# Two transformer-mixer layers on one core: VectorE's steps dealt by rank, its value products placed when ready, partial sums fetched at once

## The chip, the core and the metric

The kernel runs on one core of a Trainium2 chip. The metric is the device time of one execution in microseconds (us); lower is better. The core's engines each work through their own instructions in order and wait for one another by semaphores: TensorE (PE in the profile) multiplies matrices, ScalarE (ACT) computes activation functions, VectorE (DVE) does elementwise work and statistics, GpSimd (POOL) here computes one small power, and SyncE (SP) issues the data transfers (DMAs). Matmul results land in PSUM, all else is kept in SBUF.

## The reference

Two layers, each an attention block and a token-mixing MLP with residuals, on a sequence of 2048 tokens with 640 features:

```
def _A_ref(x, wqkv, wo):                      # H = 32 heads of Dh = 20
    q, k, v = split(x @ wqkv)                 # each (B, H, S, Dh)
    p = softmax(einsum("bhqd,bhkd->bhqk", q, k) * Dh ** -0.5)
    o = einsum("bhqk,bhkd->bhqd", p, v)
    return merge_heads(o) @ wo

def _B_ref(x, w1, b1, w2, b2):                # mixes over the 2048 tokens
    h = layernorm(x)
    u = gelu(einsum("bsd,sf->bdf", h, w1) + b1)     # F = 1536
    return transpose(einsum("bdf,fs->bds", u, w2) + b2)

x = A_x
x = x + _A_ref(layernorm(x), A_wqkv, A_wo)
x = x + _B_ref(layernorm(x), B_w1, B_b1, B_w2, B_b2)
x = x + _A_ref(layernorm(x), A_wqkv, A_wo)
x = x + _B_ref(layernorm(x), B_w1, B_b1, B_w2, B_b2)
```

(B is 1; `split`, `merge_heads` and `transpose` stand for the reshapes.) Inputs are bfloat16.

## The kernel before

**Attention (`attention`, L274).** The work of a layer is cut into 32 blocks: four query blocks of 512 queries (`qb`) by eight groups of four heads (`g`). A block has 16 units, one for each tile of 128 keys (`kt`). A unit is four chunks, one per head, each 128 keys by 512 queries. The keys 5 and 11 of every block (`D_KTS`) are VectorE's; the chunks of the other 14 units are laid end to end into tiles of three and two chunks alternately (`TW`), 717 tiles a layer.

The loop at L741 goes over these tiles and writes down the order of the instructions; nothing is reordered on TensorE or VectorE after that (`pe`, `dv` chain them). For tile `t` it emits: the scores of tile `t+1` (`emit_S`; two-chunk tiles are repeated twice, to keep TensorE busy, unless fill work is planned); ScalarE's exponential of tile `t` (`emit_exp`, L405); value products (`emit_PV`, L678) of the units whose exponentials are done; what `d_at` lists for VectorE's units; VectorE's waiting steps (`run_threads`); and matmuls of other work, the fills (`emit_fills`). Scores have two PSUM buffers, one for the three-chunk and one for the two-chunk tiles, so the scores of tile `t+2` wait for the exponential of tile `t`. The accumulator of the value products, the buffer of VectorE's scores and that of the fills (`misc`) exist once each.

**VectorE's units.** `emit_D` multiplies one chunk of scores into `Sd` and evicts it as an integer (`du<-Sd`, L416). After two chunks a thread (`d_steps`) makes the exponential of both by bit operations in three steps (`dm`, L426; `de`, L429; the product `du<-dm,du`, L433). The product of the unit with the values takes two operands, `du` and `de`. The chunks of a block's two units are emitted every second tile (`D_STEP`), and the value product six tiles after the last chunk of its unit (`D_PV_LAG`).

**Threads.** Threads are generators: each step names a cost and a delay, and `run_threads` lets them run in the order in which they were started as long as the cost fits what is left of 0.75 (`DVE_ROOM`) in the tile. `finish_thread` emits all that is left of one at once. Three kinds exist: the exponentials; the normalization of a finished block (`normalize`, L435: a transpose T out of the accumulator at once, then reciprocal, product and transpose into `attnT`; the next block's normalization finishes the thread before it emits its own T); and the layernorms of the mixer (`do_ln2`, L472: twice two statistics, mean and epsilon, a power on GpSimd, and the apply; the next token tile finishes the thread of the one before).

**Fills** are taken from a queue: key and query projections of later blocks (L254), the output projection of a finished query block (L577; that of the last query block in batches over heads 0-3, 4-6 and 7, L608), and the first mixer matmul over the tokens that are done (L552), whose partial sums go to memory (`upar`, then `uacc`). What is left of them after the last tile runs in the tail, followed by the layernorms of the last four token tiles (`emit_ln2_staged`, L503).

**Mixer (`mixer_mm1`, L782).** It multiplies the last four token tiles by their part of w1 in four passes of three 128-row groups, adds the partial sums (`ua`, fetched from `uacc` per pass into four buffers, L806; added at L833 into one of two buffers) and applies Gelu (L837). The w2 loads (L845) and the second matmul (L894) follow, in layer 0 together with the projections of the next layer.

## Time and profile before

| | us |
|---|---|
| median of 3 runs (2023.59 to 2029.77) | 2025.27 |
| profiled execution | 2016.61 |
| its span, first to last instruction | 2014.8 |

| stretch of the span (us) | length | TensorE busy | VectorE busy | ScalarE busy |
|---|---|---|---|---|
| start, projections: 0 to 47.7 | 47.7 | 34.9 | 36.6 | 25.5 |
| attention, layer 0: 47.7 to 913.9 | 866.2 | 752.8 | 601.1 | 821.4 |
| tail: 913.9 to 938.3 | 24.4 | 9.7 | 19.0 | 1.7 |
| first mixer matmul: 938.3 to 962.8 | 24.5 | 18.9 | 10.6 | 12.7 |
| second, with projections: 962.8 to 1049.5 | 86.7 | 83.7 | 49.3 | 27.8 |
| attention, layer 1: 1049.5 to 1916.3 | 866.8 | 757.5 | 601.0 | 820.5 |
| tail: 1916.3 to 1940.7 | 24.4 | 9.3 | 19.1 | 2.0 |
| first mixer matmul: 1940.7 to 1960.2 | 19.5 | 17.7 | 10.7 | 12.8 |
| second: 1960.2 to 2014.8 | 54.6 | 49.6 | 16.2 | 11.6 |

A row of a group in the profile has the line, engine and operation, what it writes and reads, shapes and count; then the busy time, the mean duration in ns, and the idle time of the engine just ahead of these instructions with what ended it. A row of the waits names the engine and line that waited, the one waited for, the total, the number of waits and the longest. A row of the timeline has the start, the duration, the instruction, and in brackets the idle time before it and its releaser. TensorE's matmuls overlap, so that rows follow each other faster than their durations.

### The profile page before, as it was taken

How to read it: one execution, taken by the hardware profiler on the slowest of the kernel's cores; microseconds unless marked ns; L12 is line 12 of the kernel's file. 1: busy time of each engine (PE TensorE's matmuls, PEld its weight loads, DVE VectorE, ACT ScalarE, POOL GpSimd, SP SyncE). 2: the span in 40 equal slices, each digit the busy share in tenths (PEclk: the TensorE clock that was granted, in tenths of full speed). 3: DMA queues.
4: the chain of work that ended last, by engine and by line, in shares of the span. 5: the costliest groups of instructions: out<-in, count | busy, mean ns of one | idle time of the engine just before them, and what ended most of it. 6: DMA issues, size and time to landing. Idle time of an engine off the chain costs nothing.

```text
span 2014.8 us, 33568 instructions
## 1 busy us (share of the span) xinstructions
PE 1734.0 (86%) x12988; PEld 624.4 (31%) x13128; DVE 1363.7 (68%) x2544; ACT 1736.2 (86%) x1575; POOL 63.2 (3%) x106
## 2 busy tenths in 40 slices
PE   7989888888898998885999898888888989888869
PEld 4222222222232322322542222222222332223235
DVE  7676668665876677766556676685668766777662
ACT  5999998999899998993339999989999999889932
POOL 2000001000000000000000000000000000000000
PEclk9999999999999999997999999999999998989979
DMA  6000000000111111234620000010001111122355
GB/s 135 1 1 1 1 11 30 1 1 1 36 47 47 47 36 57 65 93 148 208 86 1 1 1 1 17 38 1 1 1 53 54 48 42 36 74 61 104 157 180
DMA packets 113599, 96.98 MB, mean 48 GB/s; under 512 B 46752, under 2 KB 99104, under 8 KB 113440
## 3 DMA queue, kind: packets, MB, share of 16 engines
q1 hardware_dynamic: 109824, 94.82, 15.4%
q8 instruction: 102, 1.67, 0.4%
q0 software_dynamic: 3616, 0.01, 0.3%
q14 instruction: 57, 0.47, 0.1%
HBM read 63.35 MB, written 31.46 MB: 47 GB/s over the span
## 4 chain that ended last, share of the span: by engine, by line
ACT 35%; PE 30%; DVE 20%; issue 13%; DMA 1%; POOL 0%; DVEq 0%; ACTq 0%; SPq 0%; POOLq 0%
ACT P L405 35%; PE S L384 9%; PE acc L678 6%; PE y L894 5%; DVE du L416 4%; PE Sd L384 2%; PE misc L552 2%; PE misc L254 2%; PE pp L245 2%; DVE du L433 1%; DVE T L444 1%; DVE attnT L452 1%; DVE qod L223 1%; DVE qev L223 1%; DVE T L449 1%
## 5 line engine op out<-in xcount | busy, mean ns | idle before, releaser
L405 ACT ACTIVATE P<-S 128x1024 bf16<-128x1024 f32 (+1 forms) x1434 | 1642.5, 1270 | 93.0 <-PE S L384 87.3
L384 PE MATMUL S<-qev,KT 64*128 64x512 bf16 (+1 forms) x2464 | 597.7, 387 | 67.1 <-ACT P L405 53.4
L384 PE MATMUL S<-qod,KT 64*128 64x512 bf16 (+1 forms) x2376 | 586.5, 387 | 61.0 <-ACT P L405 51.3
L416 DVE TENSOR_SCALAR du<-Sd 128x512 int16<-128x512 f32 x512 | 354.2, 692 | 277.6 <-PE Sd L384 247.7
L384 PEld LDWEIGHTS <-KT 64*128 64x128 bf16 (+1 forms) x5352 | 262.5, 93 | 649.1 <-issue 573.4
L678 PE MATMUL acc<-P,Vaug 128*32 128x512 bf16 x3584 | 364.0, 395 | 23.1 <-DVE T L444 22.0
L678 PEld LDWEIGHTS <-Vaug 128*32 128x32 bf16 x4608 | 111.8, 93 | 310.0 <-issue 302.8
L433 DVE TENSOR_TENSOR du<-dm,du 128x1024 bf16<-128x1024 bf16 x256 | 177.3, 693 | 8.8
L552 PE MATMUL misc<-h2st,w1st 128*128 128x320 bf16 x576 | 127.2, 314 | 11.6 <-DVE qod L223 6.2
L192 POOL TENSOR_TENSOR rstd<-veps,mhalf 128x1 f32<-128x1 f32 x96 | 59.6, 621 | 1877.6 <-DVE veps L190 1835.0
L429 DVE TENSOR_SCALAR de<-du 128x1024 int16<-128x1024 int16 x256 | 109.3, 427 | 8.8
L426 DVE TENSOR_SCALAR dm<-du 128x1024 int16<-128x1024 int16 x256 | 109.3, 427 | 8.7
L444 DVE STREAM_TRANSPOSE T<-acc 128x512 f32<-128x512 f32 x64 | 45.9, 717 | 100.2 <-PE acc L678 97.0
L384 PE MATMUL Sd<-qod,KT 64*128 64x512 bf16 x256 | 100.5, 392 | 15.0 <-DVE du L416 14.4
L894 PE MATMUL y<-uT,w2s 128*128 128x128 bf16 (+1 forms) x753 | 106.8, 297 | 3.4 <-ACT uT L837 2.6
L384 PE MATMUL Sd<-qev,KT 64*128 64x512 bf16 x256 | 98.8, 386 | 2.6 <-DVE du L416 1.9
L254 PE MATMUL misc<-hh,wq_pad 128*128 128x512 bf16 x262 | 86.2, 396 | 12.5 <-DVE KT L639 7.0
L254 PE MATMUL misc<-hh,wk_pad 128*128 128x512 bf16 x242 | 80.4, 385 | 4.2 <-issue 2.5
L577 PE MATMUL misc<-wo_pad,attnT 128*128 128x128 bf16 (+1 forms) x363 | 74.5, 305 | 10.6 <-DVE qod L223 6.1
L552 PEld LDWEIGHTS <-w1st 128*128 128x128 bf16 x576 | 47.8, 98 | 93.0 <-issue 84.1
L894 PEld LDWEIGHTS <-w2s 128*128 128x128 bf16 x768 | 59.7, 98 | 49.0 <-issue 4.2
L678 PE MATMUL acc<-du,Vaug 128*32 128x512 bf16 x512 | 57.2, 388 | 13.6 <-DVE du L433 13.4
(91 smaller groups left out, 1027.2 us busy)
## 6 DMA issues: line engine op xcount, KB each, us to landing
w2s<-in_B_w_dram SPq DMA_DIRECT2D x16, 768.0 KB
xd<-x1s SPq DMA_DIRECT2D x24, 320.0 KB
upar<-ustg SPq DMA_DIRECT2D x48, 160.0 KB
uai<-upar SPq DMA_DIRECT2D x48, 160.0 KB
uacc<-ustg SPq DMA_DIRECT2D x48, 160.0 KB
x1in<-xd SPq DMA_DIRECT2D x24, 320.0 KB
ua<-uacc SPq DMA_DIRECT2D x24, 320.0 KB
w1st<-in_B_w_dram SPq DMA_DIRECT2D x24, 256.0 KB
```

The lines of the kernel that those rows point to most:

```text
L254: pe(nc.tensor.matmul(t[:, :], lhsT=wpad[:, dt_, g, :], rhs=st.hT[:, dt_, tb * 512:(tb + 1) * 512], start=(dt_ == 0), stop=(dt_ == NDT - 1)))
L384: pe(nc.tensor.matmul(St[:, slot, :], lhsT=KT[r0:r0 + rows, g, kt * 128:(kt + 1) * 128], rhs=q[r0:r0 + rows, :], start=True, stop=True, ti ...
L405: nc.scalar.activation(out=P[:, 0:ncs, :].rearrange("p a b -> p (a b)"), in_=St[:, 0:ncs, :].rearrange("p a b -> p (a b)"), func=ACT.Exp, ...
L416: dv(nc.vector.tensor_scalar(out=u[:, k * 512:(k + 1) * 512], in0=Sd[:, 0, :], scalar1=DBIAS, scalar2=0.0, op0=ALU.add, op1=ALU.max))
L426: dv(nc.vector.tensor_scalar(out=m[:], in0=u[:], scalar1=0x7f, scalar2=0x3f00, op0=ALU.bitwise_and, op1=ALU.bitwise_or))
L429: dv(nc.vector.tensor_scalar(out=e[:], in0=u[:], scalar1=0x7f80, scalar2=0x0001, op0=ALU.bitwise_and, op1=ALU.bitwise_or))
L433: dv(nc.vector.tensor_tensor(out=ub, in0=m[:].bitcast(BF16), in1=ub, op=ALU.mult))
L444: dv(nc.vector.transpose(out=T1[:], in_=acc[:]))
L552: pe(nc.tensor.matmul(t[:, 0:w], lhsT=states[ft]["w"][:, i, :], rhs=hts[i][:, c0:c1], start=(i == 0), stop=(i == ns - 1)))
L577: pe(nc.tensor.matmul(t[:, 0:w], lhsT=attnT[:, ttl * 128:(ttl + 1) * 128], rhs=wo_pad[:, g, c0:c1], start=(g == 0), stop=(g == NG - 1)))
L678: pe(nc.tensor.matmul(acc[32 * j:32 * j + 32, :], lhsT=Vaug[:, o:o + 32], rhs=sl[j], start=first and k3 == 0, stop=done and k3 == len(term ...
L894: pe(nc.tensor.matmul(y[:, 0:w], lhsT=w2s[:, ft, sl * 128:(sl + 1) * 128], rhs=uT[:, ft, c0:c1], start=(ft == 0), stop=(ft == NF - 1)))
```

## The change

It has four parts. Threads get a rank (exponentials 0, normalization 1, layernorm 2), and `run_threads` serves them by rank; the normalization's reciprocal becomes a step of its own, cost 0.25, and its product another, cost 0.7. The value product of VectorE's units has no fixed place: it goes into a tile in which both of the unit's threads had ended by the tile before, if that tile has fewer than three slots taken, and at the latest ahead of the block's last product. In the mixer all twelve partial sums are fetched ahead of the first pass, into twelve buffers, and the sum has three buffers in place of two. Ahead of the staged layernorms one ScalarE instruction with Gelu on one column is added.

```diff
@@ start_thread, step, run_threads
-            def start_thread(gen):
-                th = dict(gen=gen, ready=now[0], cost=0.0, done=False)
+            def start_thread(gen, rank):
+                th = dict(gen=gen, ready=now[0], cost=0.0, done=False, rank=rank, end=0)
...
                 except StopIteration:
                     th["done"] = True
+                    th["end"] = now[0]
                     threads.remove(th)
...
-                for th in list(threads):
+                for th in sorted(threads, key=lambda x: x["rank"]):
@@ normalize
-                    yield 0.9, 0
+                    yield 0.25, 0
                     dv(nc.vector.reciprocal(out=rden[:], in_=T1v[:, :, DH]))
+                    yield 0.7, 0
                     dv(nc.vector.tensor_tensor(out=T2[:], in0=T1v, ...
@@ emit_ln2_staged
+                nc.scalar.activation(out=warm[:, 0:1], in_=items[0][1][:, 0:1], func=Gelu_apprx_tanh, scale=1.0)
@@ the attention loop
-                    at_ += CFG["D_PV_LAG"]
-                    d_at.setdefault(at_, []).append(("PV", b_ * NKT + kt_, 0))
+            d_open = deque()
+            def d_done(n, before):
+                ths = [D_tiles[(n, half)][2] for half in range(2)]
+                return all(th["done"] and th["end"] <= before for th in ths)
...
                 while pv_ready and pv_ready[0][1] <= t - LAGT:
-                    emit_PV(pv_ready.popleft()[0])
+                    n_a = pv_ready.popleft()[0]
+                    if units[n_a][2] == NKT - 1:
+                        while d_open and d_open[0] < n_a:
+                            emit_PV(d_open.popleft())
+                            slots += 2
+                    emit_PV(n_a)
                     slots += 1
+                while d_open and d_done(d_open[0], t - 1) and slots < 3:
+                    emit_PV(d_open.popleft())
+                    slots += 2
                 for (op, n, i_) in d_at.get(t, ()):
-                    if op == "S":
-                        emit_D(n, i_)
-                        slots += 1
-                    else:
-                        emit_PV(n)
-                        slots += 2
+                    emit_D(n, i_)
+                    slots += 1
+                    if i_ == 3:
+                        d_open.append(n)
@@ mixer_mm1
-            uap = m1.enter_context(tc.tile_pool(name=f"uap{layer}", bufs=4))
-            tmpp = m1.enter_context(tc.tile_pool(name=f"utmp{layer}", bufs=2))
+            uap = m1.enter_context(tc.tile_pool(name=f"uap{layer}", bufs=NF))
+            tmpp = m1.enter_context(tc.tile_pool(name=f"utmp{layer}", bufs=3))
+            uas = []
+            for ft in range(NF):
+                ua = uap.tile([128, D], F32, name="ua")
+                nc.sync.dma_start(out=ua[:], in_=uacc_l[ft * 128:(ft + 1) * 128, :])
+                uas.append(ua)
             for fh in range(NPASS):
-                uas = []
-                if MMO > 0:
-                    for ftl in range(FP):
-                        ft = fh * FP + ftl
-                        ua = uap.tile([128, D], F32, name="ua")
-                        nc.sync.dma_start(out=ua[:], in_=uacc_l[ft * 128:(ft + 1) * 128, :])
-                        uas.append(ua)
```

More of the change, by code (lines that the diff above doesn't have):

```diff
@@ L39 @@
     D_STEP=2,
-    D_PV_LAG=6,
     LN_LAG=2,
@@ L420, in emit_D @@
                     D_tiles[(n, half)].append(e)
-                    D_tiles[(n, half)].append(start_thread(d_steps(u, e)))
+                    D_tiles[(n, half)].append(start_thread(d_steps(u, e), 0))
             def d_steps(u, e):
@@ L457, in steps @@
                         enqueue_outproj(qb)
-                last_th["norm"] = start_thread(steps())
+                last_th["norm"] = start_thread(steps(), 1)
             hT_dead = [False]
@@ L500, in steps @@
                         enqueue_mm1_partial(range(8, 12), uacc_l, upar_l)
-                last_th["ln"] = start_thread(steps())
+                last_th["ln"] = start_thread(steps(), 2)
             def emit_ln2_staged(items):
                 assert check_hT_dead()
+                nc.scalar.activation(out=warm[:, 0:1], in_=items[0][1][:, 0:1], func=ACT.Gelu_apprx_tanh, scale=1.0)
                 for i0 in range(0, len(items), 4):
@@ L734, in attention @@
                         d_at.setdefault(at_, []).append(("S", b_ * NKT + kt_, i_))
-                    at_ += CFG["D_PV_LAG"]
-                    assert at_ < t_end, (at_, t_end)
-                    d_at.setdefault(at_, []).append(("PV", b_ * NKT + kt_, 0))
+                assert at_ + 4 < t_end, (at_, t_end)
             LAGT = CFG["PV_LAGT"]
             pv_ready = deque((n, max(chunk_at[(n, j)][0] for j in range(4))) for n in a_units)
+            d_open = deque()
+            def d_done(n, before):
+                ths = [D_tiles[(n, half)][2] for half in range(2)]
+                return all(th["done"] and th["end"] <= before for th in ths)
             emit_S(0, 0)
@@ L762, in attention @@
                 emit_PV(pv_ready.popleft()[0])
+            assert not d_open
             finish_all()
@@ L832, in mixer_mm1 @@
                         tmp = tmpp.tile([128, D], F32, name="utmp")
-                        nc.vector.tensor_tensor(out=tmp[:], in0=big[:, ftl * D:(ftl + 1) * D], in1=uas[ftl][:], op=ALU.add)
+                        nc.vector.tensor_tensor(out=tmp[:], in0=big[:, ftl * D:(ftl + 1) * D], in1=uas[ft][:], op=ALU.add)
                         src = tmp[:]
```

## The prediction

> **What bounds the kernel now.** I read the page first, then the table of waits, then the timeline of one quiet stretch and of the disturbed ones. Both attention stages together hold 1733 of the 2015 us of the span, and in them ScalarE's exponentials are the bound.

> ```profile
> L405 ACT ACTIVATE P<-S 128x1024 bf16<-128x1024 f32 (+1 forms) x1434 | 1642.5, 1270 | 93.0 <-PE S L384 87.3
> L678 PE MATMUL acc<-P,Vaug 128*32 128x512 bf16 x3584 | 364.0, 395 | 23.1 <-DVE T L444 22.0
> ```

> ScalarE is busy for 1642.5 us and idle for 93.0 us ahead of an exponential, nearly all of it because TensorE brought the scores late. So the question of each edit in attention is: does TensorE, which works in the written order, stand still longer or shorter? The table of waits says for whom it stands still:

> ```profile
> PE acc L678 <- DVE T L444: 22.0, 26, 1.9
> PE Sd L384 <- DVE du L416: 16.3, 28, 1.3
> PE acc L678 <- DVE du L433: 13.4, 18, 1.4
> DVE h2st L197 <- POOL rstd L192: 4.4, 6, 0.8
> DVE utmp L833 <- DMA ua<-uacc: 6.6, 4, 4.7
> ```

> The first row is the accumulator that the transpose T has not yet emptied, the third is a value product that waits for VectorE's exponentials (only 18 of 128 such products wait today), the fourth a layernorm emitted in one go, the last the partial sums. Now a quiet stretch with one VectorE score tile, its steps, and the slack there is:

> ```profile
> 386.19 0.39 PE L384 MATMUL Sd<-qod,KT 64*128 64x512 bf16 x1
> 386.62 0.69 DVE L416 TENSOR_SCALAR du<-Sd 128x512 int16<-128x512 f32 x1 [1.14 <-PE Sd L384]
> 387.34 0.43 DVE L426 TENSOR_SCALAR dm<-du 128x1024 int16<-128x1024 int16 x1
> 387.60 0.37 PE L384 MATMUL S<-qev,KT 64*128 64x512 bf16 x1 [0.19 <-ACT P L405]
> 387.81 0.43 DVE L429 TENSOR_SCALAR de<-du 128x1024 int16<-128x1024 int16 x1
> 388.27 0.69 DVE L433 TENSOR_TENSOR du<-dm,du 128x1024 bf16<-128x1024 bf16 x1
> 388.35 0.09 PEld L384 LDWEIGHTS <-KT 32*128 32x128 bf16 x1 [0.42 <-issue]
> 388.94 0.37 PE L384 MATMUL S<-qod,KT 32*128 32x512 bf16 x1 [0.52 <-ACT P L405]
> ```

> ```profile
> 387.44 1.46 ACT L405 ACTIVATE P<-S 128x1536 bf16<-128x1536 f32 x1
> ```

> ```profile
> 389.67 1.48 ACT L405 ACTIVATE P<-S 128x1536 bf16<-128x1536 f32 x1
> ```

> The reader sees that the chain from the score matmul at 386.19 to the finished exponentials takes until 388.96, that TensorE is through its work at 388.35, and that the next three-bank score group runs at 388.94, as soon as its bank is free. It ends near 389.33, and the exponential that needs it starts at 389.67. With 0.10 for the handing over, 0.24 us of slack is left.

> **Part 1, value products "when ready": +115 us.** Before, the product of a VectorE tile stood six tiles behind its last score matmul. In the order of the changed program it stands two tiles behind, at all 128 places (32 blocks, 2 units, 2 layers): the planner calls a tile ready one tile after it has written down the last step. On the chip that step ends 3.6 to 4.0 us after the start of the exponential of its tile (here 388.96, the exponential having started at 385.18), and TensorE gets there earlier: after the group that began at 387.60, at 388.35. So TensorE stops until 389.02. From the first such product to the next score group the timeline has 0.53 us:

> ```profile
> 393.10 0.39 PE L678 MATMUL acc<-du,Vaug 128*32 128x512 bf16 x4
> 393.63 0.38 PE L384 MATMUL S<-qev,KT 32*128 32x512 bf16 x1
> ...
> ```

> That puts the group at 389.55 and the exponential at 390.04 instead of 389.67: 0.37 us, and 0.45 where another product stands ahead of the score matmul. Behind the waiting product there stand on TensorE, in the order listing: nothing at 24 places (0.45 each, 10.8); the next score matmul for VectorE at 24 (+0.33, the step from 385.86 to 386.19: 0.75, 18.0); one to three fill matmuls, often with that score matmul, at 80. Of these, 48 cost about 0.9 (43.2), and at 32 an eviction for a fill (0.49 to 0.75 us) stands on VectorE before the last step, so about 1.35 (43.2). Sum 115 us. Lower bound: the earliest chain (3.57 us) everywhere and the fills half hidden, 70. Upper bound: the 13.4 us of the third row left the exponentials idle for 19 us, 1.43 per us waited; on a mean wait of 0.8 us that is 146. I take 115, since it goes place by place.

> **Part 2, ranks and the split normalization: -31 us.** Before, the three steps rden, T and attnT cost 0.9 in a budget of 0.75, so they never ran by themselves; they were forced out just ahead of the next T (62 of 64 blocks). When VectorE is late, 1.66 us stand in front of T:

> ```profile
> 610.63 0.71 DVE L452 STREAM_TRANSPOSE attnT<-T 128x512 bf16<-128x512 bf16 x1
> 611.45 0.72 DVE L444 STREAM_TRANSPOSE T<-acc 128x512 f32<-128x512 f32 x1
> 612.22 0.40 PE L678 MATMUL acc<-P,Vaug 128*32 128x512 bf16 x4 [1.91 <-DVE T L444]
> ```

> Now they run one or two tiles after their own T, and no T has them in front. The 22.0 us of waits go; exponentials idled some 25 us behind them: -25 (between -29 and -18). The 13.4 us that products waited behind layernorm steps idled the exponentials for 19 us: -19. But with layernorm last, it is unfinished more often when the next token tile arrives, and is then emitted whole: 16 such runs in the listing against 6. Each holds VectorE for two statistics (0.99), mean and epsilon (0.35), the wait for GpSimd (0.73) and the apply (0.61), 2.7 us, often with 0.61 more; queued behind it are the evictions of VectorE's scores, and behind these TensorE. About half stand where a score or step is due within a tile and cost 1 to 2 us: +13 (0 to 26). Sum -31.

> **Part 3, what moves out of the tail: -12 us.** The output projection is enqueued a block earlier, so of its second batch one 128-wide group is left after the last exponential instead of all four tiles, which ran 2.22 us apart at 917.72, 919.94 and 922.16. From attnT's end (916.87) to the last batch at 924.38 that is 7.5 us less 0.5. In their place two partial-sum groups of four matmuls fall into the tail; their two additions (0.49 each) stand in VectorE's layernorm chain: +1.0. Per layer -6, both -12 (-14 to -9). In the loop, 40 fewer repeated score matmuls and 18 more projection matmuls are issued: TensorE has idle time beside them, 0; at most +3.

> **Part 4, partial sums at once, early Gelu table: -7 us.** Before, eight of twelve loads stood on SP behind three w2s loads and the reuse of four buffers; VectorE waited 4.7 us in layer 0. Layer 1, where the table load is early and the waits are 1.4 us, needs 19.4 us from its first matmul (1940.73) to its last Gelu (1960.16); layer 0 needs 24.55. Without waits 18.5 each: -6.0 and -0.9. All twelve now stand ahead of w2s and, for the last eight, behind the two additions in the tail; 3.9 MB at the 204 GB/s of that stage are 19 us, begun some 6 us before the matmuls, and each load is needed over 15 us. Should w2s come late behind them, up to 5 us are lost. The extra ScalarE instruction and table load lie in an 18 us wait: 0.

> **Sum.** +115 - 31 - 12 - 7 = +65 us. The profiled execution took 2016.6 us, so 2082 by it; the median of the runs is 8.7 us above that, so I predict 2089.

> **The clock, a cost outside the sum.** After the 1.91 us stop at 612.22 matmuls took twice as long for 3.4 us (acc at 615.37 took 0.62 us against 0.40), while stops of 0.88 and 0.96 us at 207.8 and 237.0 left them as they were. The 80 places with fills will stop TensorE for 0.8 to 1.5 us; if one in four trips the clock at about 1 us, that is +20. [...]

> **Rivals.** (a) Faster: the steps are in time. If TensorE reached each product 0.5 us later than the quiet stretch shows, the waits would be near 0.1 us and the slack of 0.24 would swallow them: 2025 - 50 = 1975. It decides where part 1 falls under 50 us, 0.39 per place. Against it: 388.35 against 388.96 is the best case for the change, not the worst. (b) Slower still: clock and layernorm runs cost their upper ends, +20 and +13 more, with part 1 at 130: 2137. For it: 1.9 us stops did cost 3.2 us of exponentials around 614. (c) The planner's order changes but the chip's does not, since everything hides in the 93 us: 2020 to 2030. Against it: the slack is in the rows, and it is 0.24 us.

> **How the numbers follow.** Forecast 0.60; (b) 0.27; (a) 0.09; (c) 0.04. The likeliest is 2089. Its own range, from part 1 at 80 to part 1 at 140, is 2055 to 2115; to leave out no more than 2 in 10 the range must take in most of (b) and the low bounds: 2040 to 2145. A measurement of this kernel tells a change from none at about 0.3%, 6 us. Faster 0.10, same 0.03, slower 0.87.

> **What would show it.** In the changed kernel's waits: the row of acc for du L433 rises from 13.4 us in 18 to about 100 us (60 to 140) in over 100; that for T L444 falls under 5 us; h2st for rstd shows some 16 waits and 11 us; utmp for DMA falls under 1 us; idle ahead of L405 rises from 93 us to 150 or more; the tail from last exponential to first big falls from 24.4 to about 18 us. Wrong it would be if the last step of VectorE's tiles ends before TensorE arrives, so that the du row stays under 30 us.

## The result, and the profile after

The changed kernel takes 2200.55 us (median of 4 runs, 2193.34 to 2211.55) against 2025.44 for the kernel before on the same chip: a ratio of 1.0866, 95% interval 1.0812 to 1.0919. It is 175 us slower. The direction was forecast, the size was not: 2089 (2040 to 2145). The profiled execution took 2193.34 us with a span of 2191.6, so it has 176.8 us more than the profiled one before (2014.8).

Almost all of it lies in the two attention stages, which grew from 866.2 and 867.3 us to 965.9 and 963.4: +195.8. The two tails shrank from 24.35 and 24.13 us (last exponential to first `big` matmul) to 17.57 and 17.57, and the first mixer matmul (to the last Gelu) from 24.54 and 19.42 us to 17.94 and 17.96. That is -13.3 and -8.1. The start took 2.4 us more.

Groups of the page, after; the last two columns are idle time just before, and what ended most of it:

```profile
L405 ACT ACTIVATE P<-S 128x1024 bf16<-128x1024 f32 (+1 forms) x1434 | 1657.4, 1257 | 273.9 <-PE S L384 268.6
L680 PE MATMUL acc<-du,Vaug 128*32 128x512 bf16 x512 | 102.6, 414 | 103.4 <-DVE du L433 102.8
```

A single exponential takes no longer than before (1257 ns in the mean, before 1270). Together they fill 1657.4 us instead of 1642.5, since they overlap less (1434 times the mean is 1802.5 us after and 1821.2 before), and ScalarE now stands idle ahead of them for 273.9 us instead of 93.0. The chain that ended last (before, then after) shows the same shift: ScalarE fell from 35% of it to 17%, VectorE rose from 20% to 34%.

```profile
ACT 35%; PE 30%; DVE 20%; issue 13%; DMA 1%; POOL 0%; DVEq 0%; ACTq 0%; SPq 0%; POOLq 0%
PE 39%; DVE 34%; ACT 17%; issue 8%; POOL 1%; DMA 0%; DVEq 0%; ACTq 0%; SPq 0%; POOLq 0%
```

The waits, after (total, number, longest):

```profile
PE acc L680 <- DVE du L433: 102.8, 100, 4.5
PE Sd L384 <- DVE du L416: 20.4, 28, 1.8
PE misc L554 <- DVE qod L222: 18.7, 14, 2.0
DVE h2st L196 <- POOL rstd L191: 11.7, 16, 0.8
PE acc L680 <- DVE T L444: 11.5, 14, 1.9
DVE utmp L844 <- DMA ua<-uacc: 4.1, 1, 4.1
```

The first row is what part 1 was to cause, and its size is as forecast. But 89 us more of these waits stand beside 181 us more of ScalarE's idle time: each microsecond that TensorE stopped cost about two. That price is the first thing that the forecast had wrong. One stretch of the timeline shows a stop in full:

```profile
407.46 0.26 DVE L448 RECIPROCAL rden<-T 128x16 f32<-128x16 f32 x1
407.82 0.75 DVE L222 TENSOR_SCALAR qev<-misc,mask_ev 128x512 bf16<-128x512 f32 x1
408.61 0.75 DVE L222 TENSOR_SCALAR qod<-misc,mask_od 128x512 bf16<-128x512 f32 x1
...
412.64 0.69 DVE L450 TENSOR_TENSOR T<-T,rden 128x512 bf16<-128x512 f32 x1
413.36 0.71 DVE L453 STREAM_TRANSPOSE attnT<-T 128x512 bf16<-128x512 bf16 x1
414.18 0.69 DVE L416 TENSOR_SCALAR du<-Sd 128x512 int16<-128x512 f32 x1
414.38 0.39 PE L680 MATMUL acc<-du,Vaug 128*32 128x512 bf16 x1
...
415.83 0.69 DVE L433 TENSOR_TENSOR du<-dm,du 128x1024 bf16<-128x1024 bf16 x1
416.57 0.40 PE L680 MATMUL acc<-du,Vaug 128*32 128x512 bf16 x3 [1.81 <-DVE du L433]
...
417.94 9.14 ACT L405 ACTIVATE P<-S 128x1536 bf16<-128x1536 f32 x8 [2.11 <-PE S L384]
```

The reader sees the normalization (reciprocal, product, transpose) and the query evictions standing on VectorE between the exponential steps of a unit whose product TensorE reached at 414.38. TensorE stands for 1.81 us, ScalarE for 2.11. The clock stayed at full speed in this stretch (granted 1.00 from 407 to 418), so these 2.11 us are the price of the stop alone.

**How the stages are compared below.** Three numbers are taken from the trace of each kernel, inside the two attention stages: their length; TensorE's *stops*, which is the sum of its gaps over 0.06 us that VectorE ended (products waiting for steps or for T, score matmuls for evictions, fills for evictions; sums of such waits in the text count the same gaps, the rows of the views only those over 0.15 us); and the *half-clock time*, the time for which the records of the granted clock show half speed. Each comparison with the kernel before uses the ratio of runs; a single profiled execution stands up to some 13 us from its median (part 1 alone 12.6 above it, the changed kernel 7.2 and the kernel before 8.8 below), so differences of under 10 us in these columns mean little.

| kernel | ratio to before (95%) | attention | stops | half-clock |
|---|---|---|---|---|
| before | 1 | 1733.5 | 87.6 | 81.9 |
| changed | 1.0866 (1.0812-1.0919) | 1929.2 | 183.2 | 252.6 |
| before + part 1 (b_pv2) | 1.0666 (1.0620-1.0711) | 1888.5 | 166.2 | 221.9 |
| the same, three tiles behind (b_pv3) | 1.0210 (1.0187-1.0232) | 1787.8 | 109.9 | 174.1 |
| before + split (b_split) | 1.0160 (1.0124-1.0195) | 1792.3 | 118.2 | 160.4 |
| before + mixer (b_mix) | 0.9967 (0.9937-0.9997) | 1734.8 | 88.1 | 78.5 |
| changed, no ranks (a_fifo2) | 1.0739 (1.0715-1.0763) | 1916.8 | 171.8 | 238.9 |
| changed, no split (a_normlate) | 1.0846 (1.0786-1.0905) | 1928.1 | 172.4 | 317.4 |
| changed + unused matmuls (a_warm2) | 1.0857 (1.0795-1.0919) | 1939.6 | 131.4 | 262.8 |
| six tiles: no ranks, no split (b_pv6m) | 0.9936 (0.9914-0.9959) | 1736.2 | 78.3 | 109.2 |
| six tiles: + split (a_fifo6) | 0.9952 (0.9929-0.9976) | 1756.9 | 106.9 | 95.6 |
| six tiles: + ranks (a_pv6n) | 0.9994 (0.9970-1.0019) | 1753.2 | 81.2 | 167.3 |
| six tiles: + both (a_pv6) | 1.0067 (1.0040-1.0094) | 1769.3 | 112.7 | 146.8 |
| b_pv6m + split, held back (b_late12) | 0.9985 (0.9968-1.0001) | 1750.4 | 85.4 | 112.6 |
| the same, normalization dealt last (b_nlast12) | 0.9880 (0.9852-0.9909) | 1731.7 | 74.2 | 116.1 |
| b_pv6m + 64 short stops (b_stopS) | 1.0202 (1.0177-1.0227) | 1788.9 | 110.2 | 174.1 |
| b_pv6m + 16 long stops (b_stopL) | 1.0286 (1.0269-1.0302) | 1803.9 | 116.2 | 194.6 |
| the same, TensorE kept running (b_stopLw) | 1.0142 (1.0097-1.0186) | 1782.7 | 83.7 | 102.4 |

### The profile page after: what moved, and what is told of

Read it like the earlier page. It is cut to its first block, busy times and chain, and to the rows that moved or that the text cites. A ratio compares the mean times of both kernels' runs of the same rounds, so it can differ in the third digit from the quotient of the medians.

```text
span 2191.6 us, 33470 instructions
## 1 busy us (share of the span) xinstructions
PE 1832.1 (84%) x12946; PEld 622.0 (28%) x13088; DVE 1362.7 (62%) x2544; ACT 1750.8 (80%) x1577; POOL 57.2 (3%) x106
## 4 chain that ended last, share of the span: by engine, by line
PE 39%; DVE 34%; ACT 17%; issue 8%; POOL 1%; DMA 0%; DVEq 0%; ACTq 0%; SPq 0%; POOLq 0%
ACT P L405 17%; PE S L384 11%; PE acc L680 9%; DVE du L416 7%; DVE du L433 5%; PE y L905 4%; PE Sd L384 4%; PE misc L253 3%; DVE de L429 3%; DVE dm L426 3%; PE misc L554 2%; PE misc L579 2%; DVE qod L222 2%; DVE qev L222 2%; DVE T L444 2%
## 5 line engine op out<-in xcount | busy, mean ns | idle before, releaser
L405 ACT ACTIVATE P<-S 128x1024 bf16<-128x1024 f32 (+1 forms) x1434 | 1657.4, 1257 | 273.9 <-PE S L384 268.6
L384 PE MATMUL S<-qev,KT 64*128 64x512 bf16 (+1 forms) x2476 | 611.8, 398 | 66.4 <-ACT P L405 55.4
L384 PE MATMUL S<-qod,KT 32*128 32x512 bf16 (+1 forms) x2324 | 599.6, 401 | 54.1 <-ACT P L405 47.3
L416 DVE TENSOR_SCALAR du<-Sd 128x512 int16<-128x512 f32 x512 | 354.2, 692 | 332.8 <-PE Sd L384 303.1
L384 PEld LDWEIGHTS <-KT 64*128 64x128 bf16 (+1 forms) x5312 | 255.5, 93 | 677.9 <-issue 609.5
L680 PE MATMUL acc<-P,Vaug 128*32 128x512 bf16 x3584 | 376.9, 410 | 11.6 <-DVE T L444 11.5
L680 PE MATMUL acc<-du,Vaug 128*32 128x512 bf16 x512 | 102.6, 414 | 103.4 <-DVE du L433 102.8
L433 DVE TENSOR_TENSOR du<-dm,du 128x1024 bf16<-128x1024 bf16 x256 | 177.3, 693 | 8.8
L384 PE MATMUL Sd<-qod,KT 64*128 64x512 bf16 x256 | 102.9, 402 | 17.8 <-DVE du L416 16.8
L429 DVE TENSOR_SCALAR de<-du 128x1024 int16<-128x1024 int16 x256 | 109.4, 427 | 8.8
L426 DVE TENSOR_SCALAR dm<-du 128x1024 int16<-128x1024 int16 x256 | 109.3, 427 | 8.7
L444 DVE STREAM_TRANSPOSE T<-acc 128x512 f32<-128x512 f32 x64 | 45.9, 717 | 106.9 <-PE acc L680 105.1
L384 PE MATMUL Sd<-qev,KT 64*128 64x512 bf16 x256 | 103.4, 404 | 3.7 <-DVE du L416 3.6
L579 PE MATMUL misc<-wo_pad,attnT 128*128 128x128 bf16 (+1 forms) x363 | 83.8, 332 | 15.0 <-DVE qod L222 6.1
L253 PE MATMUL misc<-hh,wk_pad 128*128 128x512 bf16 x252 | 87.2, 408 | 11.0 <-DVE KT L641 9.9
L222 DVE TENSOR_SCALAR qev<-misc,mask_ev 128x512 bf16<-128x512 f32 x62 | 46.6, 751 | 64.1 <-PE misc L253 59.1
L680 PE MATMUL acc<-de,Vaug 128*32 128x512 bf16 x512 | 84.1, 417 | 0.0
```

Source lines behind the costliest of these rows:

```text
L222: i = nc.vector.tensor_scalar(out=dst[:], in0=ps, scalar1=msk[:, 0:1], scalar2=None, op0=ALU.mult)
L253: pe(nc.tensor.matmul(t[:, :], lhsT=wpad[:, dt_, g, :], rhs=st.hT[:, dt_, tb * 512:(tb + 1) * 512], start=(dt_ == 0), stop=(dt_ == NDT - 1)))
L384: pe(nc.tensor.matmul(St[:, slot, :], lhsT=KT[r0:r0 + rows, g, kt * 128:(kt + 1) * 128], rhs=q[r0:r0 + rows, :], start=True, stop=True, ti ...
L405: nc.scalar.activation(out=P[:, 0:ncs, :].rearrange("p a b -> p (a b)"), in_=St[:, 0:ncs, :].rearrange("p a b -> p (a b)"), func=ACT.Exp, ...
L416: dv(nc.vector.tensor_scalar(out=u[:, k * 512:(k + 1) * 512], in0=Sd[:, 0, :], scalar1=DBIAS, scalar2=0.0, op0=ALU.add, op1=ALU.max))
L426: dv(nc.vector.tensor_scalar(out=m[:], in0=u[:], scalar1=0x7f, scalar2=0x3f00, op0=ALU.bitwise_and, op1=ALU.bitwise_or))
```

## The experiments

### Which part costs: the first four

Theory A: the place two tiles behind makes TensorE stop, and the stops halve its clock. Theory B: the ranks and the split crowd the head of the block on VectorE.

Products six tiles behind, all else as in the change:

```diff
-                while d_open and d_done(d_open[0], t - 1) and slots < 3:
+                while d_open and d_done(d_open[0], t - 5) and slots < 3:
```

> The changed kernel, with one number different: a value product of VectorE's exponentials is called ready five tiles after its last step was written down, not one, so it stands at least six tiles behind. Ranks, split normalization, tail and mixer stay as in the change. Theory A (stop and clock: the place two tiles behind makes TensorE stop, and the stops halve its clock): the waits of products for the last step fall from 102.8 us to under 15, the half-clock time inside attention from 253 us to under 90, idle ahead of the exponentials from 274 to under 110, and the time lands at 1975 (1960 to 2000), which is the old time less the 50 us of my parts 2 to 4. Theory B (crowding: with the ranks, normalization and exponential steps are pressed into the head of the block and VectorE is late for everything there): the product's wait goes, but waits for evictions and for T stay at some 40 us together and the time lands between 2030 and 2100.

Measured: 2035.3 us. The products wait no more at all, but A's 1975 is missed by 60 us: attention is 35.8 us longer than before. Something in part 2, which was to save 31 us, costs about as much. B's number holds, and so do its waits: 32.1 us for evictions of scores and 8.0 for T.

Part 1 alone on the kernel before (the `d_open` and `d_done` lines of the change, `start_thread` without a rank, the old `normalize` and mixer):

```diff
-                    at_ += CFG["D_PV_LAG"]
-                    d_at.setdefault(at_, []).append(("PV", b_ * NKT + kt_, 0))
...
+                while d_open and d_done(d_open[0], t - 1) and slots < 3:
+                    emit_PV(d_open.popleft())
+                    slots += 2
```

> The kernel before, with only the placing of the value products changed to 'when ready': steps still first come first served, normalization in one piece, old tail, old mixer. Theory A: the stops alone do it; waits of products for the last step near 100 us in about 100 places, half-clock time in attention over 200 us, time 2200 (2170 to 2240), more than the changed kernel since parts 2 to 4 are missing. Theory B: without the ranks VectorE is not crowded in the block's head, so the waits are those of the quiet stretch (50 to 75 us), and the time lands where my price of part 1 put it, 2025 + 115 = 2140 (2095 to 2165).

```profile
PE acc L679 <- DVE du L434: 75.0, 97, 1.7
PE acc L679 <- DVE T L445: 38.0, 24, 2.5
```

Measured: 2156.41 us, +135 by the ratio. Both waits and time are inside B's range (50 to 75 us, 2095 to 2165), below A's; the half-clock time, 221.9 us, is what A expected (over 200). So part 1 is most of the loss, at about its forecast price; 28 of the 103 us of product waits in the changed kernel come from the other parts. The wait for T rose too, 22.0 to 38.0 us, which no step had foreseen.

The change with the split undone:

```diff
-                    yield 0.25, 0
+                    yield 0.9, 0
                     dv(nc.vector.reciprocal(out=rden[:], in_=T1v[:, :, DH]))
-                    yield 0.7, 0
```

> The changed kernel with the normalization's split undone: its steps carry their old cost again and so run only when forced ahead of the next T. Theory B: with reciprocal and product gone from the head of the block, the waits of the first unit's products fall from 55.8 us to 30 or less, half-clock time falls by a third or more, and the time by 40 to 80 us, to about 2140. Theory A: the products' waits fall by less than 20 us, the row of acc for T rises from 11.5 us to 20 or more, and the time stays within 20 us of 2200.

Measured: 2200.99 us. The waits of the first units' products fell from 55.8 to 30.1 us, as B has it, and the time did not move, as A has it: the wait for T came back, and to 54.5 us. B was right on the waits and wrong that they would pay; the half-clock time, which B saw falling by a third, rose by 65 us.

```profile
PE acc L679 <- DVE du L433: 68.7, 86, 3.9
PE acc L679 <- DVE T L444: 54.5, 30, 3.6
```

Unused matmuls ahead of the products:

```diff
-                    emit_PV(d_open.popleft())
+                    n_d = d_open.popleft()
+                    Sx = spd.tile([128, 1, 512], F32, name="Sd")
+                    for _ in range(2):
+                        s_matmul(Sx, 0, n_d, 0, 64)
+                    emit_PV(n_d)
```

> The changed kernel with two score matmuls whose result nobody reads written ahead of each when-ready product (256 of them, about 0.4 us each at full clock, 102 us of TensorE in all), so that TensorE works where it would stand. If halving of the clock after stops carries a large part of the excess (theory A), the products' waits fall to about 35 us, half-clock time in attention falls from 253 to under 150 us, and the time falls by 20 to 60 us although work is added. If the stop itself is the whole price and the clock follows but costs nothing, the added work delays what stands behind the product at all places where the wait was shorter than 0.8 us: the time rises by 20 to 50 us.

Measured: 2198.2 us, neither a gain nor a loss, and half-clock time rose by 10 us instead of falling by 100. The products' waits fell to 40.8 us, but the waits for evictions of VectorE's scores rose from 20.4 to 30.4 us. That the added work itself made TensorE late is likely and was not shown. The run settles nothing about the clock; b_stopLw below is the better test.

### Part 2, taken apart

At six tiles behind, where no product waits, ranks and split were each taken away; the common ground is the run with neither. Without the ranks:

```diff
-                while d_open and d_done(d_open[0], t - 1) and slots < 3:
+                while d_open and d_done(d_open[0], t - 5) and slots < 3:
...
-                for th in sorted(threads, key=lambda x: x["rank"]):
+                for th in list(threads):
```

> The changed kernel with products at least six tiles behind, and in addition VectorE's steps first come first served again (no sorting by rank); the split normalization, the tail and the mixer stay. With the ranks in, this kernel took 35.8 us more in attention than the kernel before, where my part 2 had promised 31 us less. Theory L (the ranks do it: layernorm, dealt last, is emitted whole when the next token tile comes and holds VectorE): attention loses at least 25 of the 36 us, h2st's waits for rstd fall from 14.6 us to under 7, and the time is 2005 (1985 to 2015). Theory N (the split does it: reciprocal and normalization product now run in the block's head, ahead of the evictions of the query projections, and the next fill on TensorE waits for those): the time stays at 2025 to 2040 and fills still wait 30 us or more for evictions.

Without the split:

```diff
-                while d_open and d_done(d_open[0], t - 1) and slots < 3:
+                while d_open and d_done(d_open[0], t - 5) and slots < 3:
...
-                    yield 0.25, 0
+                    yield 0.9, 0
                     dv(nc.vector.reciprocal(out=rden[:], in_=T1v[:, :, DH]))
-                    yield 0.7, 0
```

> The changed kernel with products at least six tiles behind, ranks in, but the normalization in one piece again, forced ahead of the next T as before. Theory N: the waits of fills for the evictions of the query projections fall from 33.6 us to under 18, waits of acc for T come back to 20 us or more, attention is at most 15 us longer than in the kernel before, and the tail takes its old length: 2025 (2010 to 2035). Theory L: the fills wait as long as with the split, T's waits come on top, 2060 (2045 to 2075).

With neither, against the kernel before (with the other lines of `d_open` and `d_done`, and the change's lines of `mixer_mm1` and `emit_ln2_staged`):

```diff
-                    at_ += CFG["D_PV_LAG"]
-                    d_at.setdefault(at_, []).append(("PV", b_ * NKT + kt_, 0))
...
+                while d_open and d_done(d_open[0], t - 5) and slots < 3:
+                    emit_PV(d_open.popleft())
+                    slots += 2
```

> The kernel before with the new mixer part, and products placed when ready but at least six tiles behind (no ranks, normalization in one piece, old tail). It is the common ground for two runs above: against it the kernel with ranks added (2024.0) gives the price of the ranks, and the one with the split added (2013.8) the price of the split. If both do harm by themselves, as the waits of fills and of T suggest, this one is faster than either: the mixer's 7 to 9 us and the 13.4 us of product waits go, 1998 (1990 to 2008). If the harm lies only in the two together, it is level with them, 2012 to 2024.

Measured: 2013.77 us without ranks, 2023.98 without the split, 2012.73 with neither. By the ratios the ranks add 0.58% (12 us) to the last and the split 0.16% (3 us, not to be told from nothing by the intervals, but its tails are 7 us shorter in each layer and its attention stages 20.7 us longer, so that its loops have lost what the tails won); both together add 1.3%. Theories L and N are both partly right. The run with neither missed its 1998 by 15 us: half-clock time rose by 27 us while the products' waits went. The waits show where the split's promised gain is. With neither (first fence) and with the split (second):

```profile
PE acc L680 <- DVE T L445: 29.4, 29, 2.6
PE Sd L385 <- DVE du L417: 17.2, 28, 1.6
PE misc L254 <- DVE KT L641: 8.9, 14, 1.4
PE misc L554 <- DVE qod L223: 5.0, 4, 1.3
```

```profile
PE acc L680 <- DVE T L444: 4.9, 6, 1.2
PE Sd L384 <- DVE du L416: 31.9, 66, 1.8
PE misc L253 <- DVE KT L641: 15.0, 22, 1.1
PE misc L554 <- DVE qod L222: 14.9, 14, 1.8
```

T's wait fell by 24.5 us, which is the forecast's -25 to the half microsecond. The evictions of VectorE's scores rose by 14.7, and all of the fills' waits on VectorE together from 30.8 to 65.2. VectorE does the same work; the wait has changed its place, and grown.

The split alone on the kernel before, its products at their fixed six tiles:

```diff
-                    yield 0.9, 0
+                    yield 0.25, 0
                     dv(nc.vector.reciprocal(out=rden[:], in_=T1v[:, :, DH]))
+                    yield 0.7, 0
```

> The kernel before with only the normalization split in two payments (0.25 and 0.7), so that it can run by itself: no ranks, products six tiles behind, old mixer. My prediction gave this edit -25 us by the waits for T and -12 us by the tail, so 2022 - 37 = 1985 (theory L agrees: 1980 to 1995, acc for T under 8 us). Theory N: T's waits fall as well, but fills and evictions take the place: 2010 to 2030, fills wait for query evictions over 25 us against 13.9 before.

The mixer alone on the kernel before:

```diff
-            uap = m1.enter_context(tc.tile_pool(name=f"uap{layer}", bufs=4))
-            tmpp = m1.enter_context(tc.tile_pool(name=f"utmp{layer}", bufs=2))
+            uap = m1.enter_context(tc.tile_pool(name=f"uap{layer}", bufs=NF))
+            tmpp = m1.enter_context(tc.tile_pool(name=f"utmp{layer}", bufs=3))
...
+            for ft in range(NF):
+                ua = uap.tile([128, D], F32, name="ua")
```

> The kernel before with only the mixer's part: all twelve partial sums fetched at once, three buffers for the additions, the Gelu table called early. My prediction gave it -7 us, so 2015 (2010 to 2020), with utmp's 6.6 us of waits for the loads gone. If the loads are hidden anyway or crowd out the weights behind them, it is 2022 or slower. Ranks and split say nothing of this one.

Measured: 2055.24 us for the split, +32 where the forecast had -37 and theory N at most +8. Here the products, at fixed places, wait 24.5 us for their steps (13.4 before) as well. Fills wait 66.9 us for VectorE (34.7 before); The places that N named are right, its time is not. The mixer alone: 2013.81 us, 0.9967 of the time before, which is -6.7 (its interval, 0.9937 to 0.9997, is -13 to -1); the forecast's -7 fits.

### The change without ranks, and the product one tile later

The change with its products two tiles behind, without the ranks:

```diff
-                for th in sorted(threads, key=lambda x: x["rank"]):
+                for th in list(threads):
```

> The changed kernel with first come first served in place of the ranks; products two tiles behind, split, tail and mixer stay. If the prices of the parts add up, the ranks' 10 to 20 us go and it is 2185 (2170 to 2195). If the ranks do here what they are meant to do (the steps first, so that the product waits less), it is slower than the changed kernel, 2210 to 2250, with more than 110 us of product waits.

Part 1 alone (b_pv2), one tile later:

```diff
-                while d_open and d_done(d_open[0], t - 1) and slots < 3:
+                while d_open and d_done(d_open[0], t - 2) and slots < 3:
```

> The kernel before with products when ready, called ready two tiles after the last step instead of one: three tiles behind, 1.1 us later. By the arithmetic of the quiet stretch (step 0.61 us late at two tiles) the step is then 0.5 us early and TensorE stops only where an eviction or a layernorm step holds VectorE: waits of products under 25 us (75.0 at two tiles), half-clock time in attention under 130 us (222 at two), time 2040 (2020 to 2060). If VectorE is late by more than a tile in most places, the waits stay above 40 us and the time above 2070.

Measured: 2177.08 us without the ranks, in the range where the prices add up. The ranks cost the change 1.3% (1.0866 against 1.0739) even though their purpose, the steps first, is needed here most: product waits are 99.4 us without them and 102.8 with them. They don't shorten the wait that they were to shorten.

One tile later, the product's waits are 4.4 us in 6 places, as the arithmetic of the quiet stretch has it, where two tiles behind gave 75.0. But the time is 2068.62 us, above its range, and the half-clock time 174.1 where under 130 was expected: T's waits stay at 39.4 us (22.0 before) and fills wait 48.8 us on VectorE (34.7 before). So moving the product costs elsewhere too. That the product now counts as two slots in other tiles, and so shifts the fills, is a likely reason that was not tried.

```profile
PE acc L679 <- DVE T L445: 39.4, 25, 2.8
...
PE acc L679 <- DVE du L434: 4.4, 6, 1.3
```

### What a stop costs, and the clock

A product, T or fill that waits stops TensorE; the table shows attention growing by about 2 us for each microsecond of stop (+195.8 for +95.6 in the changed kernel, +155.0 for +78.6 in part 1 alone). The candidate for the other half is the clock. First, the same 46 us of VectorE work were added at T as many short or few long stops, by carrying T out several times into the same tile:

```diff
-                dv(nc.vector.transpose(out=T1[:], in_=acc[:]))
+                for _ in range(2):
+                    dv(nc.vector.transpose(out=T1[:], in_=acc[:]))
```

> The kernel with products six tiles behind, the new mixer and no ranks or split (2012.7), with the transpose T carried out twice in each of its 64 blocks: 64 times 0.72 us, 46 us of VectorE, in the middle of the place where TensorE waits. Many short stops: acc's waits for T rise from 29.5 us to 55 to 70, none over 2.8 us. If a stopped microsecond costs a microsecond (the clock is a companion), attention grows by what is added, 20 to 40 us, and the same holds for the next run. If the clock is a cause, the added half-clock time adds half of itself on top; short stops should add little of it, under 60 us, so 30 to 60 us in all.

```diff
-                dv(nc.vector.transpose(out=T1[:], in_=acc[:]))
+                for _ in range(5 if (qb * NG + g) % 4 == 1 else 1):
+                    dv(nc.vector.transpose(out=T1[:], in_=acc[:]))
```

> The same 46 us of VectorE, but as four further transposes in each fourth block only: 16 places with a stop of about 3 to 4.5 us. Stops rise by some 40 us. If the clock is a companion, attention grows by 35 to 45 us, about 1.0 per us stopped. If it is a cause, each of the 16 stops is followed by one or more windows at half speed: half-clock time grows by 55 us or more, and attention by the stops plus half of that, 70 us or more, 1.6 or more per us stopped, and more per us than with the short stops.

Measured, against the run without them: stops +31.9 and +37.9 us, half-clock +64.9 and +85.4, attention +52.7 and +67.7. A stopped microsecond costs 1.65 and 1.79; "about 1.0" is out for both. The short stops were not all short (the longest wait for T is 3.3 us, where none over 2.8 was expected). But short and long cost nearly the same, so the two did not separate the clock from a companion. The third run did: the long stops stay, and TensorE is kept running through them by repeating the score group just written.

```diff
+                    if (qb_, g_) not in pv_count and (qb_ * NG + g_) % 4 == 2 and t + 1 < NTILES:
+                        for _ in range(13):
+                            for i_, (n_s, j_) in enumerate(tiles[t + 1]):
+                                s_matmul(S_tiles[t + 1], i_, n_s, j_, 32 if TW[(t + 1) % 2] == 3 else 64)
                     emit_PV(n_a)
```

> The kernel with 16 long stops (five transposes T in each fourth block; 2079.5), with thirteen repetitions of the score group that was just written issued at those 16 places, ahead of the product that has to wait: the same scores into the same bank, 520 matmuls of about 0.4 us, two or three of them side by side, some 3 us per place. The work still stands still as long; TensorE does not, and the exponential of that group comes up to 3 us later, at a place where ScalarE would be idle for about 4. If the clock is a cause, half-clock time falls from 194.6 us to under 150, and attention by 0.4 us for each us of it, 15 to 35 us; the time is 2050 (2040 to 2068). If it is a companion, half-clock time may fall, but attention stays or grows by up to 16 us (the later exponentials): 2078 to 2096.

Measured: 2056.32 us, so 1.0142 of the time before where the same stops without the repetitions give 1.0286. Half-clock time fell from 194.6 to 102.4 us, attention by 21.2, although 520 matmuls were added. The half-clock time is then about that of the run without added stops (109.2), and the same held-up work costs 46.5 us of attention instead of 67.7: by this test the clock made up about a third of the price of the long stops, or more, if the added matmuls cost something too. With TensorE standing still (a place of the long-stop kernel):

```profile
211.90 3.72 DVE L446 STREAM_TRANSPOSE T<-acc 128x512 f32<-128x512 f32 x5
215.67 0.62 PE L681 MATMUL acc<-P,Vaug 128*32 128x512 bf16 x4 [3.88 <-DVE T L446]
216.22 0.60 PE L385 MATMUL Sd<-qev,KT 64*128 64x512 bf16 x1
...
217.48 2.53 ACT L406 ACTIVATE P<-S 128x1536 bf16<-128x1536 f32 x2 [4.37 <-PE S L385]
...
220.78 0.39 PE L385 MATMUL S<-qod,KT 32*128 32x512 bf16 x2
...
221.28 1.45 ACT L406 ACTIVATE P<-S 128x1536 bf16<-128x1536 f32 x1 [1.28 <-PE S L385]
```

and kept running (the same place of the other):

```profile
210.05 3.72 DVE L446 STREAM_TRANSPOSE T<-acc 128x512 f32<-128x512 f32 x5
...
212.84 1.02 ACT L406 ACTIVATE P<-S 128x1024 bf16<-128x1024 f32 x1 [2.50 <-PE S L385]
213.82 0.40 PE L681 MATMUL acc<-P,Vaug 128*32 128x512 bf16 x4 [1.08 <-DVE T L446]
214.15 0.39 PE L385 MATMUL Sd<-qev,KT 64*128 64x512 bf16 x1
...
214.97 3.82 ACT L406 ACTIVATE P<-S 128x1536 bf16<-128x1536 f32 x3 [1.10 <-PE S L385]
```

The five transposes last 3.72 us in both. In the first, matmuls take 0.60 to 0.62 us for 5 us afterwards, and ScalarE loses another 1.28 us at 221.28, long after the stop. In the second they take 0.39 to 0.40 at once. The stages of that time, from the view by windows (length, busy time of PE, PEld, DVE, ACT and POOL, granted clock, DMA share, GB/s), for the 5 us behind the stop, first without and then with the repetitions:

```profile
215.60:220.60 5.00, 4.93 (x19) 0.90 (x19) 3.55 (x7) 2.48 (x2) 0.00 (x0) 0.50 0.01 3
```

```profile
213.80:218.80 5.00, 4.98 (x34) 1.43 (x35) 4.31 (x7) 3.89 (x5) 0.00 (x0) 1.00 0.00 0
```

In the same 5 us TensorE is busy all the time and gets 19 matmuls done at half clock and 34 at full. So in this pair of runs the half clock came with TensorE's standing still (granted 0.50 against 1.00 in these 5 us, 194.6 against 102.4 us of half clock in attention), and it is a cause of the lost time: 21.2 us of attention came back.

### The split's steps held back

To see whether the split harms by its place, its steps were held back by twelve tiles, on the run with neither ranks nor split:

```diff
-                    yield 0.9, 0
+                    yield 0.25, 12
                     dv(nc.vector.reciprocal(out=rden[:], in_=T1v[:, :, DH]))
+                    yield 0.7, 0
```

> The same, with the normalization split and its steps held back until twelve tiles after their T, where VectorE has fewer steps of its own, instead of one tile. Theory N (the split harms by its place in the head of the block, beside the query evictions): without that place its benefits stay, T's waits fall under 8 us, fills wait no longer for query evictions than in the kernel before (about 14 us), the tail keeps 12 us less: 25 to 35 us under the run without the split, 1968 (1955 to 1985). If the split harms wherever it stands (its 1.66 us push other steps back), the time is within 8 us of the run without it, or slower.

Then they were also dealt behind the exponential steps, with rank 0 for all other threads:

```diff
-                for th in list(threads):
+                for th in sorted(threads, key=lambda x: x["rank"]):
...
-                last_th["norm"] = start_thread(steps())
+                last_th["norm"] = start_thread(steps(), 1)
```

> The kernel with the split normalization held back twelve tiles, in which 24.1 us of product waits came up because its steps stood in front of the exponential steps of the same block; here normalization alone is dealt last, behind the exponential steps, and layernorm keeps its turn. If the split costs only by pushing those steps back, product waits fall under 5 us while the waits for T stay under 5 (29.5 without the split), and the time is 1990 (1975 to 2000). If it costs by itself, by VectorE being full wherever it stands, then fills and evictions wait instead and the time is 2010 to 2025.

Measured: 2021.59 us for the first, a miss. T's waits nearly vanish, but its steps stand in front of the exponential steps, and 24.1 us of product waits appear in 12 places at the block's end, where a product is forced. For the second 1997.88 us (six runs, 1989.61 to 2008.50), within its range and 0.988 of the kernel before (0.9852 to 0.9909): the fastest here.

```profile
PE misc L580 <- DVE qod L223: 14.9, 10, 1.7
PE Sd L385 <- DVE du L417: 9.2, 10, 1.7
PE acc L681 <- DVE T L445: 8.3, 14, 1.5
```

Products wait 2.6 us, T 8.3 (under 5 was expected, 29.4 without the split), evictions of scores 9.2 (17.2 without the split); fills took part of it, 53.0 us against 30.8. Against the run with neither, the split in the block's head made attention 20.7 us longer, held back and dealt last 4.5 us shorter: most of its cost in the loops lay in what it was put in front of. The fills show that a rest stays, and the tails have lost their gain (22.49 and 23.50 us, where the split in the block's head gave 16.93 and 16.86).

## Why the forecast was right in direction and wrong in size

**Part 1, +115 (70 to 146): about right by itself.** Alone it cost 135 us by the ratio and 155 in the profiled attention stages. ScalarE's idle time inside half-clock windows rose from 28.5 to 83.4 us there; the other 100 us lie near the price that was worked out place by place, though 16 us more of waits for T, which no place counted, are in them. The row for the products, forecast at about 100 us in over 100 places, is 102.8 in 100, but part 1 alone gives 75.0 in 97 and the other 28 came with part 2: that the row hit 100 is luck.

**"The clock, a cost outside the sum", +20: the first step that failed.** It was put outside the sum and sized from "if one in four trips the clock". Measured: half-clock time in attention from 81.9 to 252.6 us, and inside these windows ScalarE is idle for 0.35 to 0.39 us in each microsecond (28.5 us before, 99.2 after), while only 6.3 us of TensorE's stops lie in them: +71 us. This gives all of ScalarE's idle time in those windows to the clock, so it is an allocation, not a test; the test, b_stopLw, got 21.2 us back for 92.2 us less of half clock, added matmuls included. The row at 615.37 had shown the half clock (granted 0.50 from 613.53 to 616.95; its 0.62 against 0.40 us is 1.55 times, not the "twice" that was read from it), and each stop was judged by its own length, against stops of 0.88 and 0.96 us that left the clock alone (granted 1.00 from 206 to 211 and from 236 to 241). In the counts below the half clock goes with the summed idle time of a window more than with its longest stop.

**Part 2, -31: wrong in sign, the second step that failed.** On top of part 1 it cost +41 us in attention (1888.5 to 1929.2), 25 without the idle time in half-clock windows. By the ratios it is more, nearly 60: the changed kernel is 2.0% (40 us) slower than part 1 alone, although its tails and mixer are some 18 us shorter. Its sub-steps: T's waits were to fall from 22.0 to under 5 us (11.5; 4.0 without the ranks) for -25; they fell by 26.5 against part 1 alone. But products wait 28 us more, fills 8 and evictions 7. What is late next when steps move was asked only for layernorm: there the 16 runs and 11 us are exactly there (16 and 11.7). For the normalization it said "now they run one or two tiles after their own T, and no T has them in front", and did not ask what they now stood in front of: query evictions and exponential steps in a stretch where VectorE has no gap (407.8 to 416.5 above). The -19 for products behind layernorm was put down to the ranks, but at six tiles these waits are gone without ranks as well as with them, by the placing alone; the ranks only cost 12 us there.

**Parts 3 and 4, -12 and -7: right.** -13.3 and -8.1 in the profile; the mixer alone -6.7. One addition still waits 4.1 us for a load where under 1 us was forecast; the lengths of the two layers, 17.94 and 17.96 us, don't show it.

**The sum**, profile against profile: 100 for part 1, 71 for the clock, 25 for part 2, -21.4 for tail and mixer, 2.4 at the start: 177, the measured 176.8. It closes by construction, since part 1 and part 2 are what is left of a difference of profiles without the clock's 71; the profile of part 1 alone was a long one for that kernel, so by the ratios some 20 us move from part 1 to part 2. The forecast had 65; of the 112 missing, the clock is 71, part 2's sign 56, and part 1 gives 15 back. (The forecast's own terms add up to 2090, not 2089.) Rival (b) named the clock but gave it 20 us, and of part 2 it doubted only the layernorm runs: 2137.

## What to carry to other kernels

When one engine feeds another in a written order, price a step by what will stand behind it, at its new place, on its own engine: a wait that is removed by moving work on a full engine comes back at the next consumer (with the split at six tiles T's waits fell by 24.5 us, and those of the fills rose from 30.8 to 65.2). Here a microsecond of TensorE's stops cost 1.65 to 2.05 us (b_stopS, b_stopL, part 1 alone, the changed kernel), part of it by the clock (in b_stopLw 21.2 of 67.7 us). Stops that fall close together are to be looked at together: in the counts below half clock went with their sum. A margin of one tile in a plan is not one tile on the chip: with one more, the products' waits fell from 75.0 us to 4.4.

## What the runs showed of the hardware

A rough fit came out of the table: in its kernels without added matmuls, the change in attention is the change in stops plus half of the change in half-clock time, within 22 us (changed: 95.6 + 85.4 = 181 for 195.8; no split: 84.8 + 117.8 = 203 for 194.6; ranks at six tiles: -6.4 + 42.7 = 36 for 19.7). Where the change is small, the miss is as large as the change, and the two kernels with added matmuls do not follow it (a_warm2: 134 for 206.1; b_stopLw: 6 for 49.2).
